# Spectral-mixer forward and backward on one core: the row stage of the 2-D transform in groups of four rows instead of two

## The chip, the cores and the metric

One core of one Trainium2 chip. The time is device microseconds (us) of one execution; medians are given with the lowest and highest run. A profiled run is about 1.8 us longer than the span that its profile shows from first to last instruction. Two kinds of time must be kept apart below: the **time of a kernel** comes from several runs, the **lines of a profile** from one execution, and one wait more or less in a profile may be that execution's own.

## The reference

The kernel computes `h2` and, for a given `grad_out`, seven gradients.

```python
h  = x + A(layernorm(x))            # A: rfft2 -> times (w_r + 1j*w_i) -> irfft2
h2 = h + B(layernorm(h))            # B: layernorm, S x F matmul, gelu, F x S matmul
# B=1, S=2048, D=448, Df=D//2+1=225, F=1792, everything stored in bf16
out, vjp = jax.vjp(f, A_x, A_w_r, A_w_i, B_w1, B_b1, B_w2, B_b2)
return (out, *vjp(grad_out))
```

## The kernel before

The 2-D transform along S and D is done with matmuls in two stages. S = 2048 is split in 16 rows by 128 partitions.

- The **row stage** takes row t: `row_a` multiplies it with a 128x128 matrix (`Rm`), `row_b` with the cosines and sines along D (`csF`, or `csB` backward). The result goes to a small buffer `cs`.
- A **reshuffle**, one DMA from SBUF to SBUF for each pair of `row_b`, writes `cs` (128 partitions) into `D2` in another order of partitions.
- The **column stage** (`s2_stage`) reads `D2[:, g]` for g = 0 to 15, one column group after the other, and multiplies it with 128x128 matrices (`Vt`, `Ut`, `Un`).

The column stage can't begin before the reshuffle that holds its first column group has landed. To have work in between, the kernel keeps generators of independent matmuls: `fill(n)` issues n steps from them. In the forward pass those are 224 steps of a gradient that needs only `grad_out` and `w2`, in the backward pass 420 steps of the two weight gradients. What is left of the backward ones at the end is issued by `drain()`, after the last inverse row. I call these matmuls **fillers**.

```python
N_FILL_B = (16, 16, 40, 8, 24, 8)
blk_ring = ring(rS, 0, 3, 8, 2, P // 2)       # 3 buffers, one for two rows
fold_ring = ring(rS, 6 * 4 * P, 4, 912)       # row_a's folded input, 4 buffers

def row_a(t, R):
    pa = ps_ff()
    ft = folds[t // 2]
    for k in range(4):
        o = DC * (4 * (t % 2) + k)
        mm(pa[:, k * P:(k + 1) * P], lhsT=ft[:, o:o + P], rhs=R, start=True, stop=True)
    if t % 2 == 0:
        blks[t // 2] = blk_ring.next()
    evac(out=blks[t // 2][:, :, t % 2, :], in_=pa[:].rearrange("p (a b) -> p a b", a=8))

def row_b(h, quarters=False):
    u, c = divmod(h, 2)
    # ... four (forward) or four half-width (backward) matmuls of blks[u] into pd ...
    # ... evac(out=cs[:, c], in_=pv)
    if c:
        defer(RESH_LAG, lambda: nc.sync.dma_start(out=D2[u:u + 121:8].rearrange("p g c k -> p (g c k)"),
                                                  in_=cs.rearrange("p x c k -> p (x c k)")), cs)

# forward row stage, cut: only the order of work on TensorE
for t in range(NT):                # NT = 16
    if t + 1 < NT: row_a(t + 1, Rs.pop(t + 1))
    fill(FILL_A[t])                # 3 each
    row_b(t - 1)
    if t == NT - 1: row_b(t)
    # ... fold_prep, statistics, loads ...
    fill(FILL_B[t])                # 3 each
fill(20)
s2_stage(...)                      # column stage

# backward, cut
def rows(t):
    if t < NT: row_a(t, Rm[:])
    fill(2)
    row_b(t - 2, True)
    fill(2)
for t in range(NT - LAG, NT + 2):  # LAG = 3; the earlier rows come earlier
    # ... loads ...
    rows(t)
fill(N_FILL_B[2])                  # 40
s2_stage(bwd_x, bwd_mult, 0, N_FILL_B[3], N_FILL_B[4], ...)
inv_rows(gx_consumer, N_FILL_B[5], aT_ring, (), True)
drain()                            # what is left of the fillers
```

In the last part, each filler step also hands out one queued VectorE or ScalarE operation of the inverse rows (`row_ops`). The backward output of the inverse rows is `gx`, stored in pieces of 224 KB.

## Time and profile before

| | before |
|---|---|
| time, median of 3 runs | 358.42 us (358.37 to 358.54) |
| span of the profiled execution | 357.2 us |
| TensorE idle in it | 15.7 us |
| end of the last matmul | 352.21 us |
| from there to the end ("tail") | 4.97 us |

The lines that carry the reading stand in the prediction below. A line of TensorE's order of time has start, length, engine, source line, operation, output<-inputs, shape, count; in brackets the idle time before it and what ended it. All matmuls have line L218 and most evictions L82, because both go through a helper; so groups are told apart by tiles: `csF` is row_b, `Rm` or `rS` by 128x128 is row_a, `Vt` is the start of a column group, `rC`, `rE`, `rO` forward and `rG`, `rst` backward are fillers.

### The profile page before, as it was taken

What the parts mean: (1) busy time and instruction counts of PE and PEld (TensorE: products, weight loads), DVE (VectorE), ACT (ScalarE), POOL (GpSimd) and SP (SyncE); (2) the same over time, 40 slices, a digit from 0 to 9 for tenths busy, and PEclk for the clock granted to TensorE, in tenths of its full rate; (3) what the DMA queues carried; (4) which work ended last, traced back from release to release, by engine and by line L of the source; (5) the groups of instructions that cost most, each with busy time, mean ns of one, the idle gap of its engine ahead of it and who ended that gap; (6) DMA issues with size and microseconds to landing.
All of it is one profiled execution on the core that took longest, in us unless ns stands there. A gap on an engine that the chain in (4) does not pass through costs nothing.

```text
span 357.2 us, 6450 instructions
## 1 busy us (share of the span) xinstructions
PE 341.5 (96%) x2133; PEld 183.8 (51%) x2133; DVE 252.5 (71%) x679; ACT 213.8 (60%) x457; POOL 67.7 (19%) x227
## 2 busy tenths in 40 slices
PE   6898998899999999999999999999999999999994
PEld 2455665555645555555555555544444444455641
DVE  5897626992884888775226978784498766499994
ACT  4669836965986545504221355565477776588883
POOL 8667000000220000001001111110000000056771
PEclk9699999999999999999999999999999999999998
DMA  8999999847999999997886999999976878999996
GB/s 207 287 200 234 200 198 162 169 140 252 280 292 336 302 348 241 252 246 218 194 192 134 192 210 194 221 175 264 264 214 201 238 196 236 245 215 221 247 286 234
DMA packets 147672, 81.62 MB, mean 229 GB/s; under 512 B 95480, under 2 KB 139768, under 8 KB 147384
## 3 DMA queue, kind: packets, MB, share of 16 engines
q1 hardware_dynamic: 147352, 80.83, 94.7%
q8 instruction: 16, 0.26, 0.3%
q10 hardware_dynamic: 288, 0.39, 0.3%
q14 instruction: 16, 0.13, 0.1%
HBM read 27.56 MB, written 23.89 MB: 144 GB/s over the span
## 4 chain that ended last, share of the span: by engine, by line
PE 79%; ACT 7%; DVE 6%; DMA 4%; issue 2%; SPq 1%; POOL 0%; ACTq 0%; DVEq 0%
PE ps_mm L218 66%; PE ps_ff L218 13%; DMA rO<-in_B_w_dram 2%; ACT rO L82 2%; DVE stats L82 2%; ACT rG L82 1%; DMA rA<-in_A_x_dram 1%; DVE r L82 1%; ACT Ut L82 1%; DVE rA L82 1%; DVE rS L82 1%; SPq L297 1%; ACT Vt L82 1%; ACT rX L82 0%; ACT rS L82 0%
## 5 line engine op out<-in xcount | busy, mean ns | idle before, releaser
L218 PEld LDWEIGHTS <-r 128*128 128x128 bf16 (+2 forms) x660 | 61.7, 104 | 49.6 <-issue 2.7
L218 PEld LDWEIGHTS <-rS 128*128 128x128 bf16 (+2 forms) x496 | 40.5, 99 | 38.3 <-issue 7.0
L218 PE MATMUL ps_mm<-rD,r 128*128 128x448 bf16 x224 | 44.5, 352 | 0.0
L82 ACT CAST rO<-ps_mm 128x512 bf16<-128x512 f32 (+1 forms) x62 | 33.5, 583 | 13.8 <-PE ps_mm L218 11.1
L218 PE MATMUL ps_mm<-rC,rE 128*128 128x448 bf16 x144 | 36.0, 369 | 3.3 <-DMA rC<-in_grad_out_dram 3.3
L218 PEld LDWEIGHTS <-rst 128*128 128x128 bf16 (+1 forms) x320 | 23.8, 97 | 29.3 <-issue 13.5
L82 ACT CAST r<-ps_ff 128x452 bf16<-128x452 f32 x58 | 33.4, 576 | 8.8 <-PE ps_ff L218 8.4
L218 PE MATMUL ps_mm<-r,rst 128*128 128x512 bf16 (+3 forms) x192 | 36.4, 353 | 0.0
L218 PE MATMUL ps_mm<-rB,r 128*128 128x448 bf16 x160 | 31.2, 352 | 0.1
L218 PE MATMUL ps_mm<-rG,rst 128*128 128x512 bf16 (+1 forms) x128 | 28.2, 380 | 0.0
L82 ACT ACTIVATE r<-ps_mm,rstd_h 128x448 bf16<-128x448 f32 x16 | 10.1, 633 | 26.1 <-PE ps_mm L218 26.1
L82 ACT ACTIVATE r<-rC 128x448 bf16<-128x448 bf16 x16 | 9.1, 572 | 26.8 <-DMA out_dram<-r 12.9
L82 DVE SCALAR_TENSOR_TENSOR r<-ps_mm,b2col,r 128x448 bf16<-128x448 f32 x16 | 10.9, 682 | 19.9 <-PE ps_mm L218 17.9
L82 DVE CAST rO<-ps_mm 128x512 bf16<-128x512 f32 (+1 forms) x18 | 11.8, 658 | 15.2 <-PE ps_mm L218 14.3
L82 ACT ACTIVATE rG<-rG 128x896 bf16<-128x896 bf16 x14 | 13.3, 950 | 14.9 <-DVE rG L82 14.6
L218 PEld LDWEIGHTS <-rO 128*128 128x128 bf16 (+1 forms) x165 | 15.6, 98 | 12.2 <-DMA rO<-in_B_w_dram 1.8
L218 PE MATMUL ps_mm<-rE,rS 128*128 128x448 bf16 x112 | 21.5, 352 | 0.0
L82 ACT CAST rG<-ps_mm 128x512 bf16<-128x512 f32 (+1 forms) x33 | 16.6, 541 | 7.3 <-PE ps_mm L218 7.2
L1180 POOL TENSOR_SCALAR lcol<-lcol 128x1 f32<-128x1 f32 x16 | 8.5, 530 | 65.1 <-ACT r L82 65.1
L218 PE MATMUL ps_mm<-rC,rO 128*128 128x448 bf16 x80 | 19.1, 352 | 1.5 <-DMA rO<-in_B_w_dram 1.5
L1371 POOL TENSOR_SCALAR lcol<-lcol 128x1 f32<-128x1 f32 x16 | 5.5, 342 | 78.5 <-ACT r L82 78.5
L218 PEld LDWEIGHTS <-rE 128*128 128x128 bf16 x148 | 14.4, 101 | 11.3 <-issue 5.0
(198 smaller groups left out, 662.6 us busy)
## 6 DMA issues: line engine op xcount, KB each, us to landing
out_dram<-rO SPq DMA_DIRECT2D x34, 256.0 KB
r<-in_B_w_dram SPq DMA_DIRECT2D x5, 1024.0 KB
r<-r SPq DMA_DIRECT2D x16, 226.0 KB
r<-r SPq DMA_DIRECT2D x32, 113.0 KB
rS<-in_B_w_dram SPq DMA_DIRECT2D x4, 896.0 KB
out_dram<-rG SPq DMA_DIRECT2D x10, 256.0 KB
rO<-in_B_w_dram SPq DMA_DIRECT2D x2, 1024.0 KB
w_d<-rG SPq DMA_DIRECT2D x1, 1808.0 KB
```

The costliest lines, as they stand in the source:

```text
L82: fn(**kw)
L218: nc.tensor.matmul(out, lhsT=lhsT, rhs=rhs, start=start, stop=stop)
L297: nc.sync.dma_start_transpose(out=wT, in_=B_w2[j * P:(j + 1) * P, :].rearrange("f (t c) -> f t c", c=P))
L1180: gp_.tensor_scalar(out=m1, in0=ms, scalar1=-1.0 / D, scalar2=None, op0=ALU.mult)
L1371: gp_.tensor_scalar(out=m1, in0=ms, scalar1=-2.0 / D, scalar2=None, op0=ALU.mult)
```

## The change

The row stage collects four rows, not two. One reshuffle then carries half of the column groups of four rows: it writes 32 partitions at a stride of four, where before it wrote 16 partitions at a stride of eight with all column groups. The count and size of the transfers stay: 8 reshuffles of 226 KB in each pass, 16 in all. The intent: the column groups 0 to 7 arrive one reshuffle earlier than 8 to 15, so fewer fillers are needed in front of the column stage (20 to 14 forward; backward 40 to 30, and four steps instead of eight beside the last rows, so that 38 steps instead of 52 stand between the last row_a and the column stage), and the write goes to twice as many partitions.

The diff, cut to its core:

```diff
-N_FILL_B = (16, 16, 40, 8, 24, 8)
+N_FILL_B = (16, 16, 30, 8, 24, 8)
     def decode(eng):                       # which row and column group a partition of D2 holds
-        floor_div(eng, a4, pcolb, 64)      # (cut: the other lines follow)
-        floor_div(eng, fc, s_, 8)
+        floor_div(eng, a4, pcolb, 32)
+        floor_div(eng, fc, s_, 4)
-    blk_ring = ring(rS, 0, 3, 8, 2, P // 2)
-    fold_ring = ring(rS, 6 * 4 * P, 4, 912)
+    blk_ring = ring(rS, 0, 2, 8, 2, 4, P // 4)
+    fold_ring = ring(rS, 8 * 4 * P, 3, 912)
     def row_a(t, R):
-        evac(out=blks[t // 2][:, :, t % 2, :], in_=pa[:].rearrange("p (a b) -> p a b", a=8))
+        evac(out=blks[t // 4][:, :, :, t % 4, :], in_=pa[:].rearrange("p (a e b) -> p a e b", a=8, e=2))
     def row_b(h, quarters=False):
-        u, c = divmod(h, 2)
+        u, e, c = h // 4, h // 2 % 2, h % 2
-            defer(RESH_LAG, lambda: nc.sync.dma_start(out=D2[u:u + 121:8].rearrange("p g c k -> p (g c k)"),
+            defer(RESH_LAG, lambda: nc.sync.dma_start(out=D2[u:u + 125:4, 8 * e:8 * e + 8].rearrange("p g c k -> p (g c k)"),
     # forward row stage
-        row_b(t - 1)
+        row_b(t - 3)
         if t == NT - 1:
-            row_b(t)
+            for i in range(t - 2, NT):
+                row_b(i)
-    fill(20)
+    fill(14)
     # backward
     def rows(t):
         if t < NT:
             row_a(t, Rm[:])
-        fill(2)
-        row_b(t - 2, True)
-        fill(2)
+            fill(2)
+        row_b(t - 4, True)
+        fill(2 if t < NT else 1)
-    for t in range(NT - LAG, NT + 2):
+    for t in range(NT - LAG, NT + 4):
```

Cut: the reordering of the tables (`fr`, `gen_R`, `Rp`) that goes with the new order of partitions.

More of the change, by code (lines that the diff above doesn't have):

```diff
@@ L356 @@
     fr = ftmp(448, 64)
-    gp_.iota(fr.rearrange("p (c i g) -> p c i g", c=2, i=4), pattern=[[1, 2], [16, 4], [2, 8]], base=0,
+    gp_.iota(fr.rearrange("p (c q i g) -> p c q i g", c=2, q=2, i=4), pattern=[[1, 2], [8, 2], [16, 4], [2, 4]], base=0,
              channel_multiplier=0, allow_small_or_imprecise_dtypes=True)
@@ L432, in gen_R @@
         t = ftmp(2688, P).bitcast(I32)
-        tv = t.rearrange("p (c h x) -> p c h x", c=2, h=2)
-        f2 = fr.rearrange("p (c x) -> p c x", c=2)
+        tv = t.rearrange("p (c h x) -> p c h x", c=4, h=2)
+        f2 = fr.rearrange("p (c x) -> p c x", c=4)
         for h in range(2):
@@ L443, in decode @@
         a4, fc, s_, c_, f_ = col(), col(), col(), col(), col()
-        floor_div(eng, a4, pcolb, 64)
-        gp_madd(s_, a4, -64.0, pcolb)
-        floor_div(eng, fc, s_, 8)
-        gp_madd(s_, fc, -8.0, s_)
-        gp_madd(s_, s_, 2.0, a4)
+        floor_div(eng, a4, pcolb, 32)
+        gp_madd(s_, a4, -32.0, pcolb)
+        floor_div(eng, fc, s_, 4)
+        gp_madd(s_, fc, -4.0, s_)
+        gp_madd(s_, s_, 4.0, a4)
         floor_div(eng, c_, fc, 4)
@@ L665, in row_a @@
             mm(pa[:, k * P:(k + 1) * P], lhsT=ft[:, o:o + P], rhs=R, start=True, stop=True)
-        if t % 2 == 0:
-            blks[t // 2] = blk_ring.next()
-        evac(out=blks[t // 2][:, :, t % 2, :], in_=pa[:].rearrange("p (a b) -> p a b", a=8))
+        if t % 4 == 0:
+            blks[t // 4] = blk_ring.next()
+        evac(out=blks[t // 4][:, :, :, t % 4, :], in_=pa[:].rearrange("p (a e b) -> p a e b", a=8, e=2))
     def row_b(h, quarters=False):
-        u, c = divmod(h, 2)
-        if u < 0 or u >= NT // 2:
+        u, e, c = h // 4, h // 2 % 2, h % 2
+        if h < 0 or h >= NT:
             return
@@ L679, in row_b @@
                 if quarters:
-                    mm(pq[:, 1 - w, b, :], lhsT=blks[u][0:DC, 2 * (2 * w + b) + c].rearrange('p j x -> p (j x)'),
+                    mm(pq[:, 1 - w, b, :], lhsT=blks[u][0:DC, 2 * (2 * w + b) + c, e].rearrange('p j x -> p (j x)'),
                        rhs=csB[0:DC, w, b, 0:KW // 2], start=True, stop=True)
                     continue
-                mm(pv[:, 1 - w, :], lhsT=blks[u][0:DC, 2 * (2 * w + b) + c].rearrange('p j x -> p (j x)'), rhs=csF[0:DC, w, b, :],
+                mm(pv[:, 1 - w, :], lhsT=blks[u][0:DC, 2 * (2 * w + b) + c, e].rearrange('p j x -> p (j x)'), rhs=csF[0:DC, w, b, :],
                    start=(b == 0), stop=(b == 1))
         if c == 0:
-            css[u] = cs_ring.next()
-        cs = css[u]
+            css[h // 2] = cs_ring.next()
+        cs = css[h // 2]
         if quarters:
@@ L900 @@
     for c in range(2):
-        sc.copy(out=Rp.rearrange("p (a q b c) -> p c a q b", c=2, q=8, a=4)[:, c],
-                in_=Rm[:, 64 * c:64 * c + 64].rearrange("p (q a b) -> p a q b", q=8, a=4))
+        for e in range(2):
+            sc.copy(out=Rp.rearrange("p (e a q b c) -> p c e a q b", e=2, c=2, q=8, a=2)[:, c, e],
+                    in_=Rm[:, 64 * c + 32 * e:64 * c + 32 * e + 32].rearrange("p (q a b) -> p a q b", q=8, a=2))
     FILL_A = (3, 3, 3, 3, 3, 3, 3, 3, 3, 3, 3, 3, 3, 3, 3, 3)
```

## The prediction

> **What bounds the kernel now.** I read the page first, then who waited for whom on TensorE, then TensorE's instructions in order of time around each place where work is held back for a transfer, and last the busy time by stage.
>
> From the page, engine totals:
>
> ```profile
> PE 341.5 (96%) x2133; PEld 183.8 (51%) x2133; DVE 252.5 (71%) x679; ACT 213.8 (60%) x457; POOL 67.7 (19%) x227
> ```
>
> TensorE is busy for 341.5 of 357.2 us, so nothing that moves no TensorE work can win more than the 15.7 us in which it is idle. Part of that is fixed: the last stretch of the stage table below (4.9 us) is the final stores, and some 4.5 us are the start. What the rest waits for, from the view of waits on TensorE:
>
> ```profile
> PE ps_mm L218 <- DMA rC<-in_grad_out_dram: 3.3, 3, 2.2
> PE ps_ff L218 <- ACT rS L82: 1.6, 1, 1.6
> PE ps_mm L218 <- DMA rO<-in_B_w_dram: 1.5, 1, 1.5
> PE ps_ff L218 <- ACT rX L82: 0.9, 1, 0.9
> PE ps_ff L218 <- DVE rS L82: 0.7, 1, 0.7
> ```
>
> The reshuffle that the change touches (D2 from cs, 16 transfers of 226 KB) is not in the list: no wait for it is visible at all. The reason is in TensorE's order of time, forward pass:
>
> ```profile
> 30.04 0.56 PE L218 MATMUL ps_ff<-csF,rS 112*128 112x226 bf16 x4 [1.61 <-ACT rS L82]
> ...
> 44.95 0.95 PE L218 MATMUL ps_ff<-csF,rS 112*128 112x226 bf16 x8
> 45.74 4.51 PE L218 MATMUL ps_mm<-rC,rE 128*128 128x448 bf16 x23
> 50.09 0.39 PE L218 MATMUL ps_ff<-permI,Vt 128*128 128x128 bf16 x4
> 50.31 0.35 PE L218 MATMUL ps_ff<-r,Vt 128*128 128x452 bf16 x1
> ...
> 60.65 0.55 PE L218 MATMUL ps_mm<-rC,rO 128*128 128x448 bf16 x2 [1.50 <-DMA rO<-in_B_w_dram]
> ...
> 68.63 0.35 PE L218 MATMUL ps_ff<-r,Vt 128*128 128x452 bf16 x1 [0.95 <-ACT rX L82]
> ```
>
> The last two row matmul groups (x8) end at 45.7; then 23 filler matmuls of the independent product run, and the first column matmul, which reads D2, starts at 50.31. The backward pass has the same shape with 48 fillers:
>
> ```profile
> 244.66 0.37 PE L218 MATMUL ps_ff<-csF,rS 112*128 112x113 bf16 x4
> 244.86 7.06 PE L218 MATMUL ps_mm<-rG,rst 128*128 128x512 bf16 x34
> 251.76 2.97 PE L218 MATMUL ps_mm<-rG,rS 128*128 128x512 bf16 x14
> 254.56 0.35 PE L218 MATMUL ps_ff<-r,Vt 128*128 128x452 bf16 x1
> ```
>
> The completion records of the trace say how tight that is. The last forward reshuffle is issued at 46.63 and complete at 50.01 (3.4 us), 0.3 us before its reader. The last backward one is issued at 248.04 and complete at 254.12 (6.1 us), 0.44 us before its reader. So the fillers hide the latency just fully, and the fillers themselves are useful work that must be done anyway.
>
> The ends of the stage table (busy time by stretch; columns are length, then PE, PEld, DVE, ACT, POOL, clock, DMA share, GB/s):
>
> ```profile
> 344.00:352.30 8.30, 8.21 (x51) 3.59 (x48) 8.16 (x25) 5.19 (x13) 4.50 (x9) 1.00 0.80 294
> 352.30:357.20 4.90, 0.00 (x0) 0.00 (x0) 0.10 (x1) 0.32 (x1) 0.00 (x0) 0.73 0.63 236
> ```
>
> TensorE runs to the end, VectorE is full beside it, and then the last stores land.
>
> [...]
> [...] the packets of the last backward reshuffle run from 252.51 to 253.26, 0.75 us, which is 309 GB/s. [...]
> [...]
> [...] the same 226 KB take 3.2 to 3.4 us when the queue is quiet and 7.0 us (issued 244.77, complete 251.78) behind two stores and a load of x.
>
> **The change part by part.** The order of instructions shows the same 2133 matmuls with the same shapes, 16 reshuffles of the same 128 pieces of 1808 bytes, and one more small copy pair on ScalarE (Rp in four pieces instead of two). Nothing is removed; things are moved.
>
> *What it buys.* The last group of four rows ends with two reshuffles. The first (column groups 0 to 7) is what the column stage needs at once; the second is needed only eight half-groups later, some 8 us forward (one each 0.95 us) and 17 us backward. So the exposed latency starts two row groups earlier, and fillers can be dropped: 23 to 17 forward, and in the backward tail from the last row_a to the column stage 60 to 44 matmuls by my count of the order.
>
> *Forward row stage, a cost.* Row groups now come two steps later. Until 30.04 TensorE waits on ScalarE and VectorE, whose order up to there is the same but for the missing evictions; the wait for the eviction of row 7 ends at 30.04 in both versions. Two row groups (0.395 us each, the step from 44.95 to 45.74 halved) that filled idle time before it now come after it: +0.79 us, and the 1.61 us wait grows to some 2.4.
>
> *Start of the forward column stage.* With that shift the four last row groups run 44.95 to 46.53, so the pair that the start needs is evicted when the last pair was before, is issued at about 46.6 and lands at about 50.0. TensorE gets there at 46.53 + 17 x 0.19 + 0.22 = 49.98. Wait: about 0 to 0.3.
>
> *The wait at 60.65.* It is for a transposed weight block, issued behind the last reshuffle and four loads; with the last issue some 0.5 us later it lands near 61.1. TensorE arrived at 59.15; now the same filler number stands two half-groups (0.38 us each) later, and 0.79 later by the row stage: 60.7. The wait falls from 1.5 to about 0.4, and at 61.1 two half-groups more are done: 0.5 - 0.77 = -0.27 us net so far. The 0.95 us wait at 68.63 (ScalarE behind the weight copies) comes when the column stage is two half-groups further; I take a third of it away: -0.3. Together forward about **-0.6 us**. The six fillers reappear in the gap before the inverse rows, which had 18 left and can now take all 24: work moved, no gain, as no wait stood there.
>
> *Backward.* All that precedes is continuous TensorE work, so the row shift costs nothing. From the last row_a (241.65, 0.4 earlier now) to the column stage took 12.91 us with 60 fillers and 3 row groups: 0.22 + 3 x 0.21 + 60 x 0.201. With 44 and 5: 0.22 + 1.05 + 8.84 = 10.1, so the reader stands at about 251.4. The pair it needs is queued right behind where the one complete at 251.78 was; in that queue 226 KB more cost 0.7 to 0.9 us, so 252.1 to 252.6. Wait: about 0.9, **+0.9 us**, for which no filler is at hand.
>
> *The end.* Fourteen filler steps move from before the column stage to the drain. VectorE's row work then ends some 3 us ahead of the last evictions, and the 224 KB store of gx issued at 351.47, whose packets stand ahead of the last four stores, is out of their way: at about 380 GB/s in that stretch, 0.6 us of queue, of which the issue times of the last stores leave **-0.3 us**.
>
> Sum: -0.6 + 0.9 - 0.3 = 0.0. I move it slightly down, to 358.1, because both filler numbers look set by trial and the backward wait is the least certain term.
>
> **The rivals.**
> *The wait returns (a).* The backward column stage starts before its half has landed, and nothing fills it: for it, the queue there is loaded (latencies of 5.5 to 7.0 us); against it, 30 looks tuned. With 2 us it makes 359.3.
> [...] every reshuffle lands earlier, the queue of 244 to 254 drains faster and both starts are free of waits: 357.0 or a little less. [...] against it the 0.75 us.
> *The four-row groups starve the row stage (c).* Two block buffers instead of three and one fold buffer fewer could make evictions wait. In program order each buffer is free one iteration before it is written, so I expect none; if it happened, 16 steps of a few tenths would make 360.
> *All is hidden (d).* Only the place of the fillers changes and the time stays at 358.4 within noise.
>
> **Range and chances.** The terms have spreads of about 0.7 (forward), 0.8 (backward) and 0.3 (end), roughly 1.1 together; 8 in 10 is 1.4 to either side: 356.7 to 359.5. Two per cent are 7.2 us, nearly half of all idle time, so faster 0.02, within 0.97, slower 0.01.
>
> **What would show it.** In the profile after: the wait on ScalarE's rS near 30 grown to about 2.4 us; the column stage at about 50.0 after 17 fillers; the wait for rO below 1 us; in the backward pass the first column matmul near 252.3 with a visible wait on a reshuffle of 0.5 to 1.5 us; a longer last run of ps_mm matmuls (62 for 46) and no gx store among the last four. I am wrong if the backward start has no wait (then the end is near 357), if the reshuffle's completion without load falls well under 3.2 us, or if row_a's evictions wait for buffers.

(Cut from it: rules for DMA transfers that no run here shows, and the gain per transfer estimated from one of them; of rival (b), its name, its condition, that the new layout makes the write much quicker, and one argument for it. No term of the sum is cut: -0.6 forward, +0.9 backward and -0.3 at the end come to 0.0 us, moved slightly down from 358.4 to 358.1. The forward and the backward term take the reshuffle to be no quicker than before: forward 3.4 us, as in the kernel before (46.63 to 50.01), and backward 0.7 to 0.9 us for 226 KB more in the queue. The latter is an estimate; the 257 GB/s that the DMA engines moved in the kernel before from 240 to 254.5 us make it 0.90 us.)

## More of the kernel before

One more view is needed for the end. This is VectorE's order of time in the kernel before, its last two lines:

```profile
351.05 0.39 DVE L82 TENSOR_TENSOR r<-r,rA 128x448 bf16<-128x448 bf16 x1
351.37 1.02 DVE L82 CAST rG<-ps_mm 128x512 bf16<-128x512 f32 x2
```

The first line is the last operation of the inverse rows. Only after it does VectorE come to the last two evictions of the fillers (CAST). From 340.3 us until then its order of time shows no idle time.

## The result, and the profile after

| | before | after |
|---|---|---|
| time, median of 3 runs | 358.42 us (358.37 to 358.54) | 357.09 us (356.56 to 357.47) |
| span of the profiled execution | 357.2 | 355.7 |
| end of the last matmul | 352.21 | 351.89 |
| tail | 4.97 | 3.79 |

Ratio after / before: 0.9961, 95% interval 0.9938 to 0.9983. Every ratio in this document is the mean time of one kernel's fast runs over that of the other's in the same rounds, so it is not quite the ratio of the medians. This is "same" at 2%, and a small real gain. The prediction had 358.1 and 356.7 to 359.5.

The engine totals of the kernel after: TensorE does the same 2133 matmuls.

```profile
PE 341.0 (96%) x2133; PEld 183.8 (52%) x2133; DVE 254.5 (72%) x680; ACT 213.6 (60%) x457; POOL 69.1 (19%) x227
```

The waits on TensorE of the kernel after (who waits, for whom: us in all, how often, the longest):

```profile
PE ps_mm L218 <- DMA rC<-in_grad_out_dram: 3.6, 3, 2.5
PE ps_ff L218 <- DVE rS L82: 1.8, 2, 1.1
PE ps_ff L218 <- ACT rS L82: 1.6, 1, 1.6
...
PE ps_mm L218 <- DMA rO<-in_B_w_dram: 0.8, 1, 0.8
...
PE ps_ff L218 <- ACT rX L82: 0.2, 1, 0.2
```

The wait for a weight block (rO) fell from 1.5 to 0.8 and that for ScalarE's rX from 0.9 to 0.2; a wait for VectorE's rS grew from 0.7 to 1.8. A wait for a reshuffle is again not in the list. TensorE's order of time, forward:

```profile
19.97 0.64 PE L218 MATMUL ps_ff<-rX,rS 128*128 128x128 bf16 x4 [1.08 <-DVE rS L82]
...
30.67 0.57 PE L218 MATMUL ps_ff<-csF,rS 112*128 112x226 bf16 x4 [1.62 <-ACT rS L82]
...
45.58 1.74 PE L218 MATMUL ps_ff<-csF,rS 112*128 112x226 bf16 x16
47.15 3.38 PE L218 MATMUL ps_mm<-rC,rE 128*128 128x448 bf16 x17
...
50.59 0.35 PE L218 MATMUL ps_ff<-r,Vt 128*128 128x452 bf16 x1
...
61.79 0.55 PE L218 MATMUL ps_mm<-rC,rO 128*128 128x448 bf16 x2 [0.78 <-DMA rO<-in_B_w_dram]
```

The last four row groups stand together (x16), 17 fillers follow, and the first column matmul starts with no wait. The wait before 30.67 is 1.62, where before it was 1.61; the 1.08 before 19.97 is new (0.12 in the kernel before). Backward:

```profile
243.80 0.37 PE L218 MATMUL ps_ff<-csF,rS 112*128 112x113 bf16 x4
244.01 7.28 PE L218 MATMUL ps_mm<-rG,rst 128*128 128x512 bf16 x35
251.13 0.35 PE L218 MATMUL ps_ff<-r,Vt 128*128 128x452 bf16 x1
```

35 fillers instead of 48, and again no wait before the column stage. By the completion records (the times at which a DMA's semaphore reaches its count), the reshuffle that holds its first groups was issued at 245.12 and complete at 250.23, 0.9 us before its reader. Forward it was issued at 47.26 and complete at 49.56: 2.30 us after its issue, and 1.0 us before its reader. The four quickest reshuffles of the kernel before took 3.2 to 3.4 us for the same bytes, those of the kernel after 2.3 to 2.4.

The end. The last lines of VectorE in the kernel after:

```profile
347.62 0.39 DVE L82 TENSOR_TENSOR r<-r,rA 128x448 bf16<-128x448 bf16 x1
347.92 0.68 DVE L82 CAST rG<-ps_mm 128x512 bf16<-128x512 f32 x1
349.44 0.69 DVE L82 CAST rG<-ps_mm 128x512 bf16<-128x512 f32 x1 [0.83 <-PE ps_mm L218]
351.60 0.76 DVE L82 CAST rG<-ps_mm 128x256 bf16<-128x256 f32 x2 [1.47 <-DMA out_dram<-rG]
```

The row work ends 3.4 us earlier than before (347.62 for 351.05), and VectorE now waits for the last matmuls instead of being behind them. The last run of matmuls, first before, then after:

```profile
344.27 7.94 PE L218 MATMUL ps_mm<-r,rst 128*128 128x512 bf16 x46
```

```profile
340.72 11.18 PE L218 MATMUL ps_mm<-r,rst 128*128 128x512 bf16 x62
```

The stage table of the kernel after in the same two stretches as before (length, then busy us and instructions of PE, PEld, DVE, ACT, POOL; clock, DMA share, GB/s):

```profile
344.00:352.30 8.30, 7.89 (x47) 3.27 (x45) 5.86 (x16) 4.18 (x9) 1.34 (x3) 1.00 0.73 278
352.30:357.20 4.90, 0.00 (x0) 0.00 (x0) 0.06 (x1) 0.00 (x0) 0.00 (x0) 0.76 0.23 82
```

In the last stretch the DMA engines move 82 GB/s where they moved 236: the stores are nearly done. The records of the last four stores say the same. Before, they were issued at 351.90, 352.37, 352.43 and 352.90 and completed between 354.08 and 355.79, behind the gx store (issued 351.47, complete 353.41). After, two of them are issued at 349.43 and 350.16, and the last two, at 352.10 and 352.60, take 1.9 us each. Counted from the last matmul, the last store is not issued earlier than before (0.69 us after it, then 0.70), but it takes 1.94 us instead of 2.89. That is 0.95 us of the shorter tail. The other 0.25 us lie between the last completion and the end of the span, a stretch that scatters from 0.9 to 1.4 us over all profiles, whatever the fillers.

So of the 1.5 us between the two profiled spans, 1.2 lie after the last matmul (4.97 to 3.79) and 0.3 before it. Whether this is more than one execution's luck, and what the reshuffle's form has to do with it, is the matter of the experiments.

### The profile page after: what moved, and what is told of

It is laid out like the page before. It is cut to its first block, busy times and chain, and to the rows that moved or that the text cites. A ratio compares the mean times of both kernels' runs of the same rounds, so it can differ in the third digit from the quotient of the medians.

```text
span 355.7 us, 6447 instructions
## 1 busy us (share of the span) xinstructions
PE 341.0 (96%) x2133; PEld 183.8 (52%) x2133; DVE 254.5 (72%) x680; ACT 213.6 (60%) x457; POOL 69.1 (19%) x227
## 4 chain that ended last, share of the span: by engine, by line
PE 73%; DVE 8%; ACT 7%; DMA 5%; issue 2%; SPq 2%; POOL 0%; DVEq 0%; ACTq 0%
PE ps_mm L218 61%; PE ps_ff L218 12%; DVE r L82 4%; DMA out_dram<-rG 2%; ACT rO L82 2%; DMA rB<-in_A_w_i_dram 2%; ACT rG L82 2%; DVE stats L82 2%; DMA rA<-in_A_x_dram 2%; SPq L297 1%; ACT Ut L82 1%; DVE rA L82 1%; DVE rS L82 1%; ACT rX L82 1%; ACT Vt L82 1%
## 5 line engine op out<-in xcount | busy, mean ns | idle before, releaser
L218 PEld LDWEIGHTS <-r 128*128 128x128 bf16 (+1 forms) x660 | 61.8, 104 | 49.6 <-issue 2.5
L82 ACT CAST rO<-ps_mm 128x512 bf16<-128x512 f32 (+1 forms) x66 | 35.2, 579 | 11.3 <-PE ps_mm L218 10.8
L82 ACT CAST r<-ps_ff 128x452 bf16<-128x452 f32 x56 | 31.8, 575 | 7.6 <-PE ps_ff L218 7.4
L1182 POOL TENSOR_SCALAR lcol<-lcol 128x1 f32<-128x1 f32 x16 | 8.5, 530 | 64.7 <-ACT r L82 64.7
L1373 POOL TENSOR_SCALAR lcol<-lcol 128x1 f32<-128x1 f32 x16 | 4.7, 296 | 77.0 <-ACT r L82 76.9
L218 PE MATMUL ps_ff<-csI,rAT 113*128 113x224 bf16 (+1 forms) x108 | 19.0, 298 | 0.6 <-ACT rAT L82 0.4
L82 ACT CAST rG<-ps_mm 128x512 bf16<-128x512 f32 (+1 forms) x28 | 14.4, 550 | 8.1 <-PE ps_mm L218 8.0
```

The source lines that it names most:

```text
L82: fn(**kw)
L218: nc.tensor.matmul(out, lhsT=lhsT, rhs=rhs, start=start, stop=stop)
L1182: gp_.tensor_scalar(out=m1, in0=ms, scalar1=-1.0 / D, scalar2=None, op0=ALU.mult)
L1373: gp_.tensor_scalar(out=m1, in0=ms, scalar1=-2.0 / D, scalar2=None, op0=ALU.mult)
```

## The experiments

**Theory P (place of the fillers).** The gain is fillers moved to the end; there they keep VectorE's row work away from the last evictions and stores. The reshuffle's new form only permits it. **Theory R (reshuffle).** The gain is the faster or earlier write itself. Under each stands a question about the reshuffle: is it the **destination** (32 partitions at a stride of four, where before it was 16 at a stride of eight) or the **early half** (column groups 0 to 7 one reshuffle ahead)?

Twelve runs (e1 and e11 are the same kernel) were made in three groups, each group on one chip and beside its own runs of the kernel before (11 runs each, medians 360.00, 358.94 and 359.86 us). Compare ratios, or medians within one group.

| group | kernel | median us | ratio to before (95%) |
|---|---|---|---|
| 1 | e1: after, unedited | 357.84 | 0.9940 (0.9908 to 0.9973) |
| 1 | e2: after, fillers put back | 359.36 | 0.9984 (0.9952 to 1.0017) |
| 1 | e3: after, 32 neighbouring partitions | 365.41 | 1.0145 (1.0114 to 1.0177) |
| 1 | e4: before, only fewer fillers | 359.75 | 0.9987 (0.9956 to 1.0018) |
| 2 | e5: before, with a probe at the end | 427.97 (1 run) | |
| 2 | e6: after, backward fillers put back | 358.08 | 0.9977 (0.9952 to 1.0001) |
| 2 | e7: after, still fewer fillers | 357.59 | 0.9959 (0.9936 to 0.9983) |
| 2 | e8: before, 14 fillers moved to the end | 358.05 | 0.9966 (0.9940 to 0.9992) |
| 3 | e9: after, 32 partitions at a stride of two | 365.82 | 1.0147 (1.0113 to 1.0182) |
| 3 | e10: after, early half made the late one | 357.62 | 0.9929 (0.9896 to 0.9963) |
| 3 | e11: after, unedited | 358.16 | 0.9939 (0.9903 to 0.9976) |
| 3 | e12: after, one weight block and five fillers earlier | 355.91 | 0.9882 (0.9850 to 0.9914) |

All gave correct results.

### e1: the kernel after, again

No edit.

> The changed kernel again, unedited, so that the others of this call have it on the same chip with more rounds. From the first result: about 1.3 us less than before (ratio 0.994 to 0.998).

Ratio 0.9940; tail 3.79 us, as in the first profile. The gain holds, and is some 0.4 to 0.6%.

### e2: the fillers put back

```diff
-N_FILL_B = (16, 16, 30, 8, 24, 8)
+N_FILL_B = (16, 16, 44, 8, 24, 8)
-    fill(14)
+    fill(20)
```

> The changed kernel with both filler numbers put back (20 forward; 44 backward, so that 52 filler steps again stand between the last row_a and the column stage). Theory A, the gain is where the fillers stand (at the end, behind VectorE's row work, and a later call for the transposed weight block): the gain goes, 358.2 to 358.9, the tail from the last matmul to the end is again near 5 us instead of 3.8. Theory B, the gain is the faster reshuffle itself: stays near 357.1.

(Theories A and B of this expectation are P and R here.) Ratio 0.9984, an interval that holds 1, and 1.5 us over e1 in the medians of the same rounds: most of the gain is gone, with the new reshuffle untouched. The last run of fillers is again that of the kernel before, 46 matmuls, and VectorE's last evictions again come right after its row work:

```profile
353.78 0.39 DVE L82 TENSOR_TENSOR r<-r,rA 128x448 bf16<-128x448 bf16 x1
354.08 1.02 DVE L82 CAST rG<-ps_mm 128x512 bf16<-128x512 f32 x2
```

They end at 355.1, 1.7 us after the last matmul (353.40), and the tail is 6.50 us. The profiled execution was the slowest of the six (361.68 us), so the size is not to be taken as typical, the order is: here VectorE's row work ends 0.77 us after the last matmul, in the kernel before 0.76 us ahead of it, and the last store is issued 2.21 us after the last matmul instead of 0.69. That makes the 1.5 us by which this tail is longer than the 4.97 of the kernel before. This speaks for P and against R.

### e3: the same write into 32 neighbouring partitions

```diff
-        floor_div(eng, a4, pcolb, 32)      # decode: 5 lines
-        gp_madd(s_, a4, -32.0, pcolb)
-        floor_div(eng, fc, s_, 4)
-        # (cut)
+        floor_div(eng, s_, pcolb, 8)
+        gp_madd(fc, s_, -8.0, pcolb)
-            ... out=D2[u:u + 125:4, 8 * e:8 * e + 8] ...
+            ... out=D2[32 * u:32 * u + 32, 8 * e:8 * e + 8] ...
```

> The changed kernel with another row layout in D2: each reshuffle still writes 32 partitions in four pieces of 1808 bytes, but 32 neighbouring ones[...]. Theory P, [...] the latency goes from 2.3 back to 3.2 us; the backward column stage then waits up to 0.5 us and the time rises by 0.2 to 1 us over the changed kernel. Theory N, the number of partitions (or of pieces per partition) sets it: latency stays at 2.3 us and the time as in the changed kernel.

(Theory P of this expectation is that the choice of destination partitions makes the write slower, not the P of this section.) The direction came as expected, the size did not: 1.0145, and 7.6 us over e1 in the same rounds, where 0.2 to 1 us were expected. The waits on TensorE and the two places, forward and backward:

```profile
PE ps_ff L218 <- DMA r<-r: 7.6, 2, 5.9
```

```profile
55.79 0.54 PE L218 MATMUL ps_ff<-r,Vt 128*128 128x452 bf16 x1 [5.87 <-DMA r<-r]
...
259.71 0.36 PE L218 MATMUL ps_ff<-r,Vt 128*128 128x452 bf16 x1 [1.73 <-DMA r<-r]
```

`r<-r` is the reshuffle. The waits add up to the whole loss. The reshuffles took 3.6 to 10.8 us from issue to completion, and in the forward pass one packet took 0.24 us in the median, where it takes 0.08 in the kernel after. Same bytes, same packets, same number of partitions, same early half: the choice of destination partitions alone is worth more than all that the change won.

### e4: the kernel before with as few fillers

```diff
-N_FILL_B = (16, 16, 40, 8, 24, 8)
+N_FILL_B = (16, 16, 26, 8, 24, 8)
-    fill(20)
+    fill(14)
```

With 26 the steps between the last row_a and the column stage are 38, as in the kernel after.

> The kernel before with the filler numbers of the change alone (14 forward; backward 38 filler steps from the last row_a to the column stage). Both readers then come before their reshuffle has landed: waits of about 0.8 us forward and 2.5 us backward. If fillers alone made the gain (theory A without the reshuffle), the tail still shortens by 1.2 us and the sum is 359.5 to 360.5; a time at or below 357.5 would say that the new layout is not needed at all.

0.9987: nothing won. The tail is short (3.62 us), so the end is won, but the wait that the fillers had hidden comes back in the backward pass:

```profile
253.34 0.35 PE L218 MATMUL ps_ff<-r,Vt 128*128 128x452 bf16 x1 [2.03 <-DMA r<-r]
```

Forward, a wait of 0.6 us appears before the column stage:

```profile
50.26 0.35 PE L218 MATMUL ps_ff<-r,Vt 128*128 128x452 bf16 x1 [0.63 <-ACT VTt L82]
```

The profile puts it down to ScalarE's table VTt; the reshuffle landed at 50.12, so it would have cost nearly as much. With e1 beside it this compares the two reshuffles, and the orders of rows that go with them, at equal filler numbers: 359.75 against 357.84 us, 1.9 us, about the visible wait. So R is half right: the new reshuffle is needed to spend fewer fillers in front of the column stage.

### e5: a probe of the write alone

24 transfers of the reshuffle's size at the end of the kernel before, into a buffer that nobody reads any more; each waits for the one before.

```diff
+    for _ in range(4):
+        for a, b, st in ((0, 121, 8), (0, 125, 4), (0, 32, 1), (0, 16, 1), (0, 127, 2), (0, 61, 4)):
+            n = (b - a + st - 1) // st
+            nc.sync.dma_start(out=r3[a:b:st, 0:904 * (128 // n)], in_=rX[:, 0:904])
```

> The kernel before with 24 extra transfers after its last store, one at a time, each of 128 pieces of 1808 bytes from one row of every partition, into six sets of partitions in turn: 16 at a stride of eight ([...]the shape of before), 32 at a stride of four ([...]the shape after), 32 neighbours[...] 16 neighbours[...], 64 at a stride of two[...], 16 at a stride of four[...] If the number of partitions counts instead: first, fourth and sixth alike, second and third alike. [...]

The second to fourth repeats agree within 0.05 us; the table has their medians.

| destination | issue to completion | first packet's start to last packet's end |
|---|---|---|
| 32 partitions, stride 4 (after) | 2.26 us | 0.74 us |
| 64 partitions, stride 2 | 2.28 | 0.75 |
| 16 partitions, stride 8 (before) | 2.84 | 1.11 |
| 16 partitions, stride 4 | 2.82 | 1.12 |
| 32 neighbours (e3) | 3.64 | 1.19 |
| 16 neighbours | 3.88 | 1.36 |

In all shapes the first packet starts 1.21 to 1.25 us after the issue. Before to after is 0.58 us of a quiet transfer. The number of partitions does not decide it alone: 32 took 2.26 or 3.64 us, 16 took 2.82 to 3.88. Why one set is quicker than another is not shown. And the view of packets shows only a part: to 32 neighbours, the packets take 0.45 us longer than at a stride of four, the completion 1.38. The completion, for which the next transfer waits, came some 0.3 us after the last packet's recorded end at 32 partitions by four, and 1.2 us after it at 32 neighbours.

### e6: only the backward fillers put back

```diff
-N_FILL_B = (16, 16, 30, 8, 24, 8)
+N_FILL_B = (16, 16, 44, 8, 24, 8)
```

> The changed kernel with only the backward filler number put back (44 for 30; forward stays 14). By the run with both put back (1.5 us above the changed kernel in the same rounds): if the backward fillers and the tail carry it, this run is 1.0 to 1.5 us above the changed kernel (about 0.9984 of before) with a tail above 4.8 us; if the forward ones do, it stays within 0.4 us of the changed kernel (about 0.994 of before).

0.9977, tail 4.75 us. Neither branch of the expectation came out clean: the ratio lies between the two, and its interval overlaps with that of e1 and ends at 1.0001. In the same group its median (358.08 us) is that of e8 below (358.05), which has the short tail. The run fits P and does not test it: differences of 0.2% can't be told apart here.

### e7: still fewer fillers

```diff
-N_FILL_B = (16, 16, 30, 8, 24, 8)
+N_FILL_B = (16, 16, 26, 8, 24, 8)
-    fill(14)
+    fill(10)
-    s2_stage(fwd_x, fwd_mult, ML_F, 3, 24, True)
+    s2_stage(fwd_x, fwd_mult, ML_F, 3, 28, True)
```

> The changed kernel with still fewer fillers: 10 forward (four more go to the gap before the inverse rows) and 26 backward. The reshuffles landed 1.0 us (forward) and 0.9 us (backward) before their readers, so no wait should come back. If the wait for the transposed weight block (0.8 to 1.0 us) shrinks by two more half-groups, 0.5 to 0.8 us less than the changed kernel; if the tail has nothing more to give, not more than that; if a wait comes back, the same or slower.

0.9959 with a tail of 3.57 us: no better than the kernel after. The weight block's wait is down to 0.3 us. No wait for a reshuffle came back, but well inside the forward column stage TensorE waits 0.38 us for ScalarE's rX and 0.78 for VectorE's r, and 0.61 before the inverse rows. The last need not come from the edit: e11, the kernel after unedited, waits 1.51 us there. Going on in this direction gained nothing.

### e8: the end alone, in the kernel before

The reshuffle and all that leads to the column stage stay as before; the backward column stage takes one filler less in each of its 20 half-groups and six more after it. Net 14 fillers go to the end.

```diff
-N_FILL_B = (16, 16, 40, 8, 24, 8)
+N_FILL_B = (16, 16, 40, 7, 30, 8)
```

> The kernel before, its reshuffle and its row stages untouched, with 14 filler steps moved from the backward column stage to the drain at the end (7 instead of 8 per half-group, and 30 instead of 24 in the gap after). If the shorter end comes from VectorE's row work lying earlier against the last matmuls, the tail falls from 5.0 to about 3.7 us and the time by 1.0 to 1.5 us (0.996 to 0.997 of before). If the end is short only because the new reshuffle frees the DMA queue, nothing changes (0.999 to 1.001).

0.9966 from two numbers: 0.3%, where the whole change gave 0.4 to 0.6%, with overlapping intervals (the kernel after unedited did not run in this group). Its end is that of the kernel after, 62 fillers in the last run and VectorE waiting for a matmul:

```profile
339.34 11.17 PE L218 MATMUL ps_mm<-r,rst 128*128 128x512 bf16 x62
```

```profile
348.06 0.69 DVE L82 CAST rG<-ps_mm 128x512 bf16<-128x512 f32 x1 [0.77 <-PE ps_mm L218]
```

Tail 4.02 us. This is P's strongest support: most of the gain, if not all, is to be had without the new reshuffle, if fillers are taken where they hide nothing. The profiled execution is the fastest of the six (356.32 us). Of the 2.7 us between its span and that of the kernel before, 0.95 lie in the tail, and 1.50 are the wait for the weight block, with which the edit has nothing to do. That shows how far one profile can be trusted: the 1.50 us wait for the weight block, of which the prediction made much, is not there in e8's execution and is 1.02 us in e5's, although the forward code of both is that of the kernel before.

### e9: 32 partitions at a stride of two

```diff
-            ... out=D2[u:u + 125:4, 8 * e:8 * e + 8] ...
+            ... out=D2[64 * (u // 2) + u % 2:64 * (u // 2) + u % 2 + 63:2, 8 * e:8 * e + 8] ...
```

(with `decode` to match). The 32 partitions lie within one half of the 128, as in e3, but no two are direct neighbours.

> The changed kernel with a third row layout in D2: each reshuffle writes 32 partitions at a stride of two inside one half of the 128[...]. The run with 32 neighbours was 7.6 us slower, but alone such a transfer took 3.65 us where 16 partitions at a stride of eight[...] took 2.84. [...] If neighbours are all of it: between the two, 3 us or more above. If neither matters here: as the changed kernel.

(Cut from the expectation: a cause that no run here shows, and the branch that rested on it, with 0.3 to 1.5 us above the kernel after; "neither" is that cause and neighbours.) My expectation missed. 1.0147, as slow as e3 and 7.7 us over e11:

```profile
PE ps_ff L218 <- DMA r<-r: 7.2, 2, 6.3
```

Latencies run from 3.7 to 11.2 us. So it is not neighbourhood that makes e3 slow. The kernel before, with 16 partitions, has 3.2 to 8 us and is far from this. The kernel after has the same number of partitions and the same half-groups as e9 and is not slow either. What e3 and e9 have alone is 32 partitions that all lie within one half of the 128. The probe's 16 partitions at a stride of four lie within one half too and were as quick as those of the kernel before (2.82 and 2.84 us), and its 64 at a stride of two, over all 128, were as quick as those of the kernel after (2.28 and 2.26 us); but the probe ran without load, and it did not have e9's shape. What of the layout it is, and why it costs 7 us under load, was not settled.

### e10: the early half made late

```diff
-        u, e, c = h // 4, h // 2 % 2, h % 2
+        u, e, c = h // 4, 1 - h // 2 % 2, h % 2
```

Now column groups 8 to 15 go first, and the column stage needs the last reshuffle.

> The changed kernel with the two halves of column groups in the other order, so that the reshuffle the column stage needs first is the last one issued[...]. In the changed kernel that last one landed at 50.64 and 251.74, its first reader of the other half came at 50.59 and 251.13. If the early half is what lets the fillers go, waits of 0.1 to 0.5 us forward and 0.5 to 1 us backward come, and the time rises by 0.5 to 1.3 us; if the faster write alone is enough, nothing changes within 0.3 us.

0.9929, no slower than e11 (0.9939) in the same rounds. Its traces are small. Backward there is

```profile
251.45 0.35 PE L218 MATMUL ps_ff<-r,Vt 128*128 128x452 bf16 x1 [0.17 <-DMA r<-r]
```

and forward the view shows no wait, but the first column matmul starts 0.40 us after the matmuls before it began, where it is 0.22 in the kernel after; its reshuffle had landed at 50.51, 0.14 us before it. So the early half, which the prediction took for the source of the spare fillers, is worth about 1 us of slack in each pass (its reshuffle landed 1.0 and 0.9 us before the reader), but at these filler numbers its loss costs only 0.2 us in each pass, and nothing shows in the time (to the 0.4% that the intervals leave). With e4 this leaves the quicker write as what lets the fillers go.

### e11 and e12: is more to be had?

e11 is the kernel after, unedited, as the partner of e12.

> The changed kernel unedited, as the comparison for the others of this call: 1.3 to 2.1 us below the kernel before (0.994 to 0.9965).

0.9939, tail 3.80 us: the third profile of the same kernel, and the third tail of 3.8.

e12 lets one more transposed weight block be loaded during the row stage (the cap on them goes from 8 to 9) and puts five fillers in front of the row_a that waits for VectorE's rS.

```diff
-CAP = 8
+CAP = 9
-    FILL_B = (3, 3, 3, 3, 3, 3, 3, 3, 3, 3, 3, 3, 3, 3, 3, 3)
+    FILL_B = (3, 3, 8, 3, 3, 3, 3, 3, 3, 3, 3, 3, 3, 3, 3, 3)
```

> The changed kernel with what is left in its forward row stage taken up: five fillers more after the third row, where matmuls wait 1 us for VectorE, and one transposed weight block asked for before the spectral weights instead of after, so that the next one no longer keeps TensorE waiting (0.8 to 1.0 us). If both waits are pure loss: 1.0 to 1.8 us below the changed kernel (0.990 to 0.992 of before). If the earlier block only pushes the reshuffles back in the queue: waits at the column stage, and no gain.

0.9882: 355.91 us (355.50 to 357.10), faster than both kernels, 0.6% below e11 in the same rounds. Both waits that it aimed at are gone from its view of waits; what remains in the forward column stage is

```profile
PE ps_ff L218 <- ACT rX L82: 1.2, 1, 1.2
```

so a part came back as a wait for ScalarE, which had been 0.25 in e11. The gain over e11, 2.25 us in the medians, is more than the two waits were there (0.85 and 0.79); where the rest comes from is not shown. The two edits were not run apart.

## Why the prediction was right or wrong

The time was right: 358.1 predicted, 357.09 measured, within the range, and "same" had 97%. Part of that is luck. The predicted change was -0.3 us and the measured one -1.3; 357.09 is the number of rival (b), 357.0. Two of the three signs that the prediction named for being wrong came: no wait at the backward start, and a reshuffle well under 3.2 us without load (2.3). The mechanism was right in one term, the end. Of the other two, the backward one did not come and the forward one is not shown.

- **The end, -0.3 us: right in mechanism, too small.** It measured -1.2 us. The term counted only the queue behind one gx store. What it left out is VectorE: before, its last two evictions had to wait for the row work and were issued together, so that the gx store and all four last stores went out within 1.4 us. After, three of these five are issued 1.7 us or more ahead of the last matmul. The profiles with 46 matmuls in the last run (before, e2, e6) have tails of 4.97, 6.50 and 4.75 us, and a last store of 2.9 us; the ten with 62 or 64 (all others but the probe) have 3.57 to 4.02 us, and a last store of 1.93 to 1.99 us, whatever their time and their reshuffle.
- **Is the tail where the time came from?** By the traces, yes, as far as a profile tells. From the first inverse-row matmul of the forward pass to the last matmul, the kernel before takes 265.6 us, e8 also, and the three profiles of the kernel after take 265.5 to 265.7: nothing was won there. e2 loses most of the gain by putting the fillers back, and e8 gets 0.3% in the kernel before. But in the three comparisons of the two kernels the medians differ by 1.3 to 2.2 us, more than the tail does; where the rest lies is not shown.
- **The backward wait, +0.9 us: did not come.** The first column matmul stood at 251.13, near the 251.4 of the prediction, but the reshuffle was complete at 250.23 instead of 252.1 or later. The step that failed is to take the reshuffle to be no quicker than before. It rested on a packet width of 0.75 us in one transfer of the kernel before, read as 309 GB/s and so as proof that the destination does not matter. It was the narrowest: the other ten of that kernel whose packets stand apart from those of the next spread over 0.97 to 3.31 us. The probe shows a width of 1.11 us for that layout when alone, and more time after the packets. Rival (b), a quicker write, was right, with 0.58 us alone and 1.9 us under load (e4 against e1). What makes the new layout quicker is not shown.
- **Forward row stage, +0.79 us: right in sum, wrong in place.** The waits there went from 2.26 to 3.24 us, +0.98. But the wait at 30 did not grow (1.61, 1.62); the loss is the 1.08 us before the fifth row_a, which waits for VectorE's folded input. In program order two row groups (0.79 us) stood before it and now come later, so the step "filled idle time before and come after it now" held, at a place that I had not looked at, because its wait of 0.12 us before was not in the list. In other executions of the same row stage this wait is 0 (e7) to 1.46 us (e10). The sum is steadier: the wait at 30 ends on average at 30.0 us with the row stage of the kernel before (four profiles) and at 29.9 with the new one (nine), so at the same time in both, as the prediction said, and with the new one two row groups fewer are done by then.
- **Forward column stage at 50.0 without much wait: right**, with 50.59. The first fillers alone started 0.57 us later in this execution (9.22 for 8.65).
- **The weight block, from 1.5 to 0.4 us, and ScalarE's rX, a third off:** 0.8 and 0.2 us. The direction was right; as the first varies between 0 and 1.5 us with the same forward code, one execution could not carry a term of this size, in either direction.
- **Forward in sum, -0.6 us: not shown.** From the first filler to the first inverse-row matmul, the forward code of the kernel before took 77.9, 77.7 and 76.3 us (before, e5, e8), that of the kernel after 77.0, 77.7, 78.7 and 77.2 (after, e1, e11, e6). The scatter is larger than the term.
- **The early half as the source of the spare fillers: not needed** at these filler numbers, by e10.
- **Rival (c), starved buffers:** TensorE shows no new wait for an eviction into a block buffer; e2, with the same buffers, is not slower than before. **Rival (d), no change in time:** the place of the fillers did change the time, a little.

Open are three things: what slows the layouts of e3 and e9 (up to 10.8 and 11.2 us for a reshuffle) while other transfers run, where the gain beyond the tail lies, and why VectorE fell behind in e2's execution.

## What to carry to other kernels

Where independent work hides a latency, the place of each piece is a choice with two sides: look also at what it would hide elsewhere, above all at the end, where here the last evictions and stores came behind VectorE's row work (a tail of 4.97 us, and of 3.79 without that). Before a transfer is made earlier by restructuring the code, try its destination layout: the same bytes to other partitions moved this kernel by 2% (7.6 and 7.7 us, e3 and e9). And don't judge a transfer by the width of its packets; take issue to completion: in the probe a width greater by 0.45 us went with a completion later by 1.38.
